# A decode kernel whose planner no longer puts filler matmuls into the two banks of the weighted sum

## The chip, the cores and the metric

The kernel runs on one core of a Trainium2 chip. The metric is the device time of one execution in microseconds. Three runs of the kernel before gave 1105.93, 1108.88 and 1117.53 us; their median, 1108.88 us, is the time before.

## What is computed

Eight batch rows, one token each, go twice through an attention layer A over a key and value cache and a small MLP block B, each with a residual sum. A's cache and weights are the same in both rounds.

```python
x = x + A(layernorm(x), k_cache, v_cache, wq, wo)
x = x + B(layernorm(x), w1, w2, w3, w4)
x = x + A(layernorm(x), k_cache, v_cache, wq, wo)
x = x + B(layernorm(x), w1, w2, w3, w4)
# A: q = x @ wq (16 heads of 256); k, v: [8 rows, 8 heads, 4096, 256], a head serves two query heads
#    p = softmax(q @ k.T / 16);  o = p @ v;  out = o @ wo
# B: h = gelu(layernorm(x) @ w1), shifted along the sequence in four groups, then @ w2 -> x1
#    x1 + gelu(layernorm(x1) @ w3) @ w4
```

All tensors are bf16; x is 8 x 448. The sequence has length one, so the shift in B brings in zeros alone, and the kernel reads neither w1 nor w2.

## The kernel before

**Data.** One head of one row has 2 MB of keys and 2 MB of values. Each such tile is cut into four quarters of 512 KB, with 128 partitions of 4 KB. The SBUF buffer `kv` has 30 places for quarters (`QUARTERS`). SyncE issues every load of keys and values (L622); one transfer brings one to four neighbouring quarters. A load waits until the last reader of each of its places is done. Between the two rounds of one row the kernel keeps the keys of five heads and six quarters of values on the chip, so these aren't read twice.

**A front and a back for each head.** `front` does the keys: TensorE transposes each half quarter with four fp32 transposes into one of the four PSUM banks psT0 to psT3 (L1219), VectorE or ScalarE copies the bank back over the same half quarter (L1202, L1203), and then the scores are made with the transposed keys as weights (L1037, 16 matmuls per quarter, the query column repeated to 48 columns). The maximum, the exponential and the sum follow on VectorE, GpSimd and ScalarE. `back` does the values: the weighted sum, eight matmuls per quarter (L1104), goes into columns 0 to 255 of one of two banks, psP0 and psP1, which the backs use in turn. VectorE then rounds the result and takes the remainder (L1118, L1120). A small matmul adds the four partial sums into columns 256 to 259 of the same bank (L1128), VectorE scales them to `oT` (L1134), and four matmuls multiply by the head's rows of wo (L1153). Columns 264 to 511 of psP0 and psP1 hold nothing that the result needs: here they are the upper halves.

**The stretch between a row's rounds.** After the last head of round one, a row goes through a chain that can't be split: psR to SBUF (L1163, L1165), the turn (L979, L982), the last head's product with wo, the sums of the norm, the MLP's two products (L833, then L979 and L982 again), the new queries (L817), and then the scores of round two. Meanwhile the values of the next row's three heads that keep nothing come in through the few places of `kv` that are free. The last two key quarters of head 7 don't stay in `kv`. They are held in transposed form in the four psT banks (`held_banks`, `HOLD = 2`), from their transposes in round one until head 7's scores in round two.

**The planner.** All work is listed as operations with durations, and `Plan.schedule` plays it through on a model: it orders each engine's instructions, gives places in `kv` to loads, and joins neighbouring quarters into one transfer. The order it finds is written out as the fixed instruction order of each engine, with semaphores. When the model finds TensorE idle, it may put in fillers: matmuls of the identity by itself, whose result nobody reads. They keep TensorE active. Over a sliding 3.413 us it aims at 3,500 columns (`TARGET`), and a filler is placed only where it is over before the next TensorE operation starts in the model. A filler needs a PSUM bank that is empty by the model's record, `bank_ev`: an operation with the attribute `tbank` set to a bank marks it occupied if it is a TensorE operation, and otherwise enters itself as the one that emptied it. Of the banks that are not occupied, the one that was emptied first is taken, and the filler waits for the operation that emptied it.

```python
b = [(x.end if x else -1.0, k) for k, x in bank_ev.items() if x is not True]
b = min(b, default=(1e9, 0))
if b[0] + 0.1 > u or u < 20.0:
    u += 0.1
    continue
f = self.filler(b[1])
...
if o.tbank is not None:
    bank_ev[o.tbank] = True if e == "pe" else o
```

For psT the marks are set in `transpose_piece`: occupied by the transposes, emptied by the copy, where a held piece's copy comes only in round two. For psP they are set in `back`: occupied by the first quarter's weighted sum, emptied by the operation that writes `oT`. The function `filler` makes 512 columns in a psT bank and 248 in the upper half of a psP bank. A bank that never gets a mark is never a candidate.

## Time and profile before

| | before |
|---|---|
| median of three runs | 1108.88 us |
| the profiled execution, its own time | 1107.5 us |
| its span, first to last instruction | 1105.7 us |
| mean granted TensorE clock | 0.927 |
| TensorE busy, of the span | 970.7 us, 88% |
| VectorE, ScalarE, GpSimd busy | 52%, 26%, 9% |
| HBM read | 438.38 MB, 396 GB/s over the span |
| DMA engines busy for the SyncE queue | 97.2% |
| fillers in the upper halves of psP | 184 of 248 columns, 35.6 us busy |
| fillers in psT | 42 of 512 columns, 14.5 us busy |

### The profile page before, as it was taken

To read this page: it belongs to the slowest core of one execution; us is meant where nothing else is said; L and a number is where in the kernel's file an instruction comes from. 1 tells how busy PE (TensorE), PEld (TensorE's weight loads), DVE (VectorE), ACT (ScalarE), POOL (GpSimd) and SP (SyncE) were. 2 spreads that over 40 slices of the span, in tenths; PEclk is the share of its full clock that TensorE was granted. 3 is DMA by queue.
4 is the path that set the end of the run, shared out by engine and by line. 5 is a ranking of instruction groups with operands and counts; after the bars stand their busy time and mean duration, and the time that the engine had idled before them with its cause. 6 is when DMAs were issued, how large, how long until landed. Compare 5 with 4: busy or idle time off the path is not lost.

```text
span 1105.7 us, 42629 instructions
## 1 busy us (share of the span) xinstructions
PE 970.7 (88%) x19504; PEld 775.8 (70%) x19504; DVE 572.6 (52%) x1782; ACT 287.7 (26%) x844; POOL 97.6 (9%) x275
## 2 busy tenths in 40 slices
PE   4889889898899988998988898998889898899987
PEld 4668657785678856786666865778567785688674
DVE  4345445554455544655544554565545655356644
ACT  1133113331224302242122321233112331234120
POOL 0000010010100101010000100100010100101010
PEclk9899989998899979999888989999979999799998
DMA  9999999999999999999999999999999999999994
GB/s 333 406 426 420 391 392 424 424 421 388 400 422 425 419 355 426 423 424 420 368 424 426 419 359 358 423 425 416 393 396 424 424 404 388 413 416 398 360 408 178
DMA packets 54543, 441.13 MB, mean 399 GB/s; under 512 B 5838, under 2 KB 9052, under 8 KB 27100
## 3 DMA queue, kind: packets, MB, share of 16 engines
q1 hardware_dynamic: 54356, 438.41, 97.2%
q8 instruction: 153, 2.51, 0.9%
q14 instruction: 26, 0.21, 0.0%
q10 hardware_dynamic: 8, 0.00, 0.0%
HBM read 438.38 MB, written 0.01 MB: 396 GB/s over the span
## 4 chain that ended last, share of the span: by engine, by line
PE 56%; DMA 32%; SPq 4%; issue 4%; DVE 3%; ACT 1%; POOL 0%
PE psT L1219 20%; DMA kv<-in_A_k_cache_dram 19%; PE psM L1037 16%; DMA kv<-in_A_v_cache_dram 13%; PE psP L1104 9%; SPq L622 4%; PE psR L1153 4%; PE psM L817 2%; PE psP L1424 1%; PE psP L1128 1%; PE psM L979 1%; DVE oS L1120 1%; DVE oS L1118 1%; PE psM L982 1%; ACT pT L1071 1%
## 5 line engine op out<-in xcount | busy, mean ns | idle before, releaser
L1219 PE MATMUL psT<-ident_f,kv 128*128 128x128 f32 x2816 | 388.6, 284 | 24.0 <-DMA kv<-in_A_k_cache_dram 23.3
L1202 DVE COPY kv<-psT 128x512 f32<-128x512 f32 x415 | 284.1, 690 | 176.5 <-PE psT L1219 170.0
L1219 PEld LDWEIGHTS psT<-ident_f,kv 128*128 128x128 f32 x2816 | 312.0, 144 | 48.4 <-DMA kv<-in_A_k_cache_dram 28.8
L1203 ACT COPY kv<-psT 128x512 f32<-128x512 f32 x321 | 186.5, 585 | 386.1 <-PE psT L1219 385.4
L1104 PE MATMUL psP<-kv,pT 128*2 128x256 bf16 x4096 | 187.5, 293 | 30.7 <-issue 16.9
L1037 PEld LDWEIGHTS psM<-q2T,kv 128*128 128x128 bf16 x4096 | 129.9, 100 | 46.7 <-issue 34.8
L1037 PE MATMUL psM<-q2T,kv 128*128 128x48 bf16 x4096 | 145.3, 189 | 13.2 <-issue 10.8
L1037 PEld LDWEIGHTS psM<-q1T,kv 128*128 128x128 bf16 x4096 | 134.3, 97 | 17.5 <-issue 11.2
L1037 PE MATMUL psM<-q1T,kv 128*128 128x48 bf16 x4096 | 143.2, 184 | 1.1 <-issue 0.4
L1104 PEld LDWEIGHTS psP<-kv,pT 128*2 128x2 bf16 x4096 | 79.1, 84 | 72.0 <-issue 27.3
L1071 ACT ACTIVATE pT<-sS,nb,fac 128x32 bf16<-128x32 f32 x128 | 52.7, 417 | 242.5 <-DVE nb L1065 242.5
L1061 POOL PARTITION_ALL_REDUCE gm<-pm x128 | 45.5, 355 | 758.3 <-DVE pm L1059 710.2
L1056 DVE COPY sS<-psM 128x64 f32<-128x64 f32 x128 | 28.5, 223 | 107.9 <-PE psM L1037 105.2
L1118 DVE CAST oS<-psP 128x256 bf16<-128x256 f32 x128 | 53.9, 421 | 51.4 <-PE psP L1104 49.2
L1153 PE MATMUL psR<-wo_sb,oT 128*1 128x448 bf16 x448 | 68.7, 390 | 5.0 <-DVE oT L1134 2.0
L1075 POOL PARTITION_ALL_REDUCE Db<-rs x128 | 51.0, 398 | 215.6 <-ACT pT L1071 215.6
L1128 PE MATMUL psP<-sel,oS 128*128 128x2 bf16 x512 | 32.4, 167 | 33.0 <-DVE oS L1120 29.2
L1128 PEld LDWEIGHTS psP<-sel,oS 128*128 128x128 bf16 x512 | 25.4, 100 | 49.8 <-DVE oS L1120 41.4
L1071 ACT ACTIVATE pT<-sS,nb 128x32 bf16<-128x32 f32 x128 | 40.9, 326 | 68.7 <-DVE nb L1065 68.7
L1120 DVE TENSOR_TENSOR oS<-psP,oS 128x256 bf16<-128x256 f32 x128 | 54.1, 423 | 3.5
L817 PEld LDWEIGHTS psM<-x2c,wq_sb 128*128 128x128 bf16 x768 | 30.7, 98 | 18.5 <-DVE sS L1056 6.1
L817 PE MATMUL psM<-x2c,wq_sb 128*128 128x24 bf16 x768 | 36.6, 184 | 5.0 <-issue 4.3
(159 smaller groups left out, 574.5 us busy)
## 6 DMA issues: line engine op xcount, KB each, us to landing
kv<-in_A_k_cache_dram SPq DMA_DIRECT2D x72, 2048.0 KB, 20.1
kv<-in_A_v_cache_dram SPq DMA_DIRECT2D x54, 2048.0 KB, 17.6
kv<-in_A_v_cache_dram SPq DMA_DIRECT2D x125, 512.0 KB, 7.5
kv<-in_A_v_cache_dram SPq DMA_DIRECT2D x54, 1024.0 KB, 10.7
kv<-in_A_k_cache_dram SPq DMA_DIRECT2D x23, 1024.0 KB, 12.2
kv<-in_A_v_cache_dram SPq DMA_DIRECT2D x5, 1536.0 KB, 10.2
kv<-in_A_k_cache_dram SPq DMA_DIRECT2D x12, 512.0 KB, 7.6
wo_sb<-in_A_wo_dram SPq DMA_DIRECT2D x1, 3584.0 KB, 45.5
```

Source lines behind the costliest of these rows:

```text
L817: last = t.matmul(bank[:, at + i * step:at + i * step + copies], w, r, start=(kc == 0), stop=(kc == 3))
L1037: last = t.matmul(ps[:, SB + 2 * i:SB + 2 * i + 2 * REP], a[:, c:256:2], bcast(rhs(c), REP, 1), start=(c == 0), stop=(c == 1))
L1071: return a.activation(pT[nr][:, :, :].rearrange("p i j -> p j i")[:, jj, :], sview[:, jj, :], ACT.Exp, bias=nb[nm][:, jj:jj + 1], scale=sc ...
L1075: plan.op("pool", lambda gp: gp.partition_all_reduce(Db[nr][:, :], rs[nr][:, :], P, RO.add), 0.5, "sum", rd=[("rs", nr, 0), ("rs", nr, 1)] ...
L1104: last = t.matmul(ps[g4:g4 + 2, PV0:PV0 + DH], pT[nr][:, i, :], slot_ap(q, s * 256, 256), start=(i < 4), stop=(i >= 28), skip_group_check= ...
L1118: plan.op("dve", lambda v: v.tensor_copy(oS[:, 0, :], po), 0.36, "o", rd=[("pv", par, x) for x in range(4)], wr=["oS0"], banks=[bk], prio=hi)
L1120: plan.op("dve", lambda v: v.tensor_tensor(oS[:, 1, :], po, oS[:, 0, :], ALU.subtract), 0.36, "o", rd=["oS0"] + [("pv", par, x) for x in r ...
L1128: last = t.matmul(ps[:, PV1 + 2 * c:PV1 + 2 * c + 2], oS[:, w, c:DH:2], sel[:, :], start=(w == 0), stop=(w == 1))
L1153: last = t.matmul(psR[r:r + 1, 0:D], oT[no][:, i % 2, i // 2:i // 2 + 1], wo_sb[:, a:a + D], start=(k == 1 and i < 2), stop=(k == HKV - 1 ...
L1202: return e.tensor_copy(dst, psT[bank][:, :])
L1203: return e.copy(dst, psT[bank][:, :])
L1219: last = t.transpose(psT[bank][:, s * P:(s + 1) * P], src, ident_f[:, :])
```

## The change

Both marks in `back` are taken away, so psP0 and psP1 never enter the planner's record of banks, and fillers can go only into psT0 to psT3. Nothing else is edited: the function `filler` still has its branch for psP, which is no longer reached. The schedule is made anew with the same model, targets and durations.

```diff
@@ back
                     wr=[("pv", par, x) for x in range(u, 4)], banks=[bk])
-            if u == 0:
-                o.tbank = bk
             if u not in keep_v:
                 o.frees = vs[u]
@@ back
         plan.op("dve", lambda v: v.tensor_tensor(
             oT[no][:, :, :], ps[:, PV1:PV1 + 4].rearrange("p (c j) -> p c j", c=2),
             bcast(rc[nr][:, :], 2, 1), ALU.mult), 0.16, "o", rd=[("o2", par), ("rc", nr)],
-            wr=[("oT", no)], banks=[bk], prio=hi).tbank = bk
+            wr=[("oT", no)], banks=[bk], prio=hi)
```

## The prediction

> **What bounds the kernel now.** I read the page's slices first, then the span cut into stretches, then the fillers, and last TensorE's own order around them. The page's slices and the chain that ended last:

> ```profile
> PEclk9899989998899979999888989999979999799998
> DMA  9999999999999999999999999999999999999994
> GB/s 333 406 426 420 391 392 424 424 421 388 400 422 425 419 355 426 423 424 420 368 424 426 419 359 358 423 425 416 393 396 424 424 404 388 413 416 398 360 408 178
> PE 56%; DMA 32%; SPq 4%; issue 4%; DVE 3%; ACT 1%; POOL 0%
> ```

> The DMA engines are busy nearly everywhere, yet the rate falls from some 424 to some 360 GB/s eight times, and the clock is low nearby. These are the stretches between the rounds of a row. Cut there, busy time of each engine, clock, DMA share and GB/s:

> ```profile
> 119.00:150.00 31.00, 26.87 (x587) 18.26 (x587) 13.42 (x60) 2.76 (x11) 1.15 (x3) 0.89 0.99 376
> 652.00:685.00 33.00, 27.50 (x598) 17.28 (x595) 15.77 (x70) 3.03 (x12) 1.86 (x5) 0.84 0.89 328
> 416.00:521.00 105.00, 92.46 (x1838) 77.25 (x1838) 58.07 (x155) 31.76 (x92) 10.90 (x29) 0.98 1.01 424
> ```

> The eight stretches (from 119, 257, 390, 521, 652, 786, 921 and 1023 us; 228 us in all) run at 360 GB/s on average, the seven between them (709 us) at 420. So 228 x (1 - 360/420) = 33 us of transfer are lost in the stretches, 1.9 to 7.2 us in each. Outside them the kernel is bound by transfers; inside, by how fast TensorE frees the few places for values. The change can only matter inside, because that is where the fillers are:

> ```profile
> L1424 PE MATMUL psP<-ident_f x184: 272/274/412, 119.4 to 1042.4; 128*128 128x248 bf16 x184
> ```

> ```profile
> L1424 PE MATMUL psP<-ident_f x43: 272/274/408, 119.4 to 140.8; 128*128 128x248 bf16 x43
> ```

> The second line is the first stretch alone. Cut as above, the filler line has 168 instructions in the eight stretches, all in psP: the 42 in psT stand before 119 us (24), after 1086 us (15) and three between.

> **Removed: are the fillers gone or moved?** In the first stretch the last transposes start at 114.75 us, and the next copies out of psT come at 147.5 to 149.1 us, on both engines, with no transpose between: all four psT banks are held. A held bank is marked occupied, so the planner has no bank at all and places nothing there. I count 168 of the 184 as gone. The 16 outside the stretches, in groups of one to three, can go to psT, at 512 columns where two of 248 stood; I cost that at nothing, since the transfers run at 420 GB/s there and cover TensorE, and at a filler's 0.1 to 0.2 us each, 3 us at most, if they didn't.

> **Removed: TensorE time.** A psP filler takes 9 per 1.20 us at full clock (row at 258.77), 10 per 2.25 us at half. That is some 20 to 35 us of TensorE, but nearly every group ends in a wait: the instruction after it starts within 0.05 us of the semaphore that it waits for, in all but a few of the groups. The clear exception:

> ```profile
> 522.64 2.25 PE L1424 MATMUL psP<-ident_f 128*128 128x248 bf16 x10
> 524.81 0.42 PE L1104 MATMUL psP<-kv,pT 128*2 128x256 bf16 x8
> ```

> Here the weighted sum waits for nothing but the fillers, 2.2 us. I take -2.0 us (bounds 0 and -3, with the few single fillers at 0.1 to 0.2 us).

> **Added: half-clock windows.** Cut on the clock's grid of 3.413 us, TensorE's idle time in a window stands against the clock of the next. Over the whole span, 20 windows have at least 1.5 us idle and 16 of them are followed by half clock; of the 260 with under 0.9 us, 21 are. Now two windows with fillers, as they are, and below them the fillers alone:

> ```profile
> 388.39:391.81 3.42, 2.61 (x30) 1.50 (x30) 2.09 (x7) 0.72 (x4) 0.40 (x1) 1.00 0.98 386
> 391.81:395.22 3.41, 2.55 (x69) 1.71 (x70) 1.17 (x4) 0.00 (x0) 0.00 (x0) 1.00 1.00 400
> ```

> ```profile
> 388.39:391.81 3.42, 1.69 (x12) 1.02 (x12) 1.00 0.98 386
> 521.51:524.93 3.42, 2.60 (x12) 1.29 (x10) 0.50 1.00 414
> ```

> Without fillers the window at 388.39 is idle for 3.42 - 2.61 + 1.69 = 2.5 us, and 391.81 should fall to half clock. The same sum gives 1.9 to 2.8 us at 118.74, 125.57, 255.27, 258.69, 521.51, 784.34 and 787.75, each followed by full clock today: eight candidates, at 16 in 20 some 6.4 new windows, 22 us at half clock on top of the 161 that the whole run has (twice the mean clock's shortfall, 2 x 0.073 x 1105.7). In the windows that follow stand 212 weighted-sum matmuls (0, 16, 32, 16, 40, 48, 20 and 40) and six matmuls of wo rows (L1153). The price of a weighted sum at the two clocks:

> ```profile
> 261.06 1.04 PE L1104 MATMUL psP<-kv,pT 128*2 128x256 bf16 x32 [0.35 <-DMA kv<-in_A_v_cache_dram]
> ```

> ```profile
> 659.54 1.88 PE L1104 MATMUL psP<-kv,pT 128*2 128x256 bf16 x32
> ```

> (1.88 - 1.04)/32 = 26 ns each, 5.5 us; four wo rows go from 0.54 us (258.29) to 0.91 us (521.79), so six cost 0.5. The MLP's product L833, 56 matmuls, takes 1.56 us at half clock (132.21) and 1.55 at full (529.72): nothing. Together 6.0 us if all is on the path, and 0 if waits for values hide it, as DMA waits hide much there. I take half: +3.0.

> [...]

> **Moved: the order.** The planner replays everything with a colder model clock, so loads can be cut and placed differently. The trace has no such second plan. The nearest rows are the stretches themselves, which do the same work in other orders: they lose 3.8, 4.1, 3.6, 7.2 and 3.7 us (from 257, 390, 521, 652, 786). The dear one:

> ```profile
> 654.63:658.05 3.42, 2.97 (x19) 0.50 0.92 352
> 658.05:661.46 3.41, 3.41 (x49) 0.50 1.02 418
> 661.46:664.87 3.41, 2.78 (x66) 1.00 0.13 55
> ```

> Clock, DMA share and GB/s end these lines. After two windows at half clock the weighted sums run late, no place comes free, and the transfers stop (0.13). One stretch turning from 3.6 to 7.2 costs +3.6; the bounds are -3.6 (that one mends) and +3.6 in each of seven. I take one: +3.6, since more half clock leans that way.

> **Sum.** 1107.5 - 2.0 + 3.0 + 3.6 = 1112.1 us for a profiled execution; with the 1.4 us by which the median stands above it, 1113.5 us, 0.4% slower. The three runs before spread over 1.0%, so a change within 1% (1098 to 1120) is about what cannot be told from none.

> **The rivals.**

> *Slower by more.* The stop of 661.46 becomes common: half clock in the stretch, weighted sums late, the free places not emptied, transfers standing. For it: in SyncE's waits, loads of L622 wait for weighted sums (L1104) 148 times, 373.6 us in all. Against: the stretches at 257, 390 and 521 have 10 to 14 us of half clock each (twice the shortfall of 0.80, 0.74 and 0.79) and no such stop. Full cold price, no gain from the fillers and three more such stretches: 1107.5 + 6.0 + 3 x 3.6 + 1.4 = 1126 us. It decides from two stops on with the full cold price: 6.0 + 7.2 is over 1%.

> [...]

> *It does nothing.* The planner finds psT banks after all in the stretches, and puts as many columns there: 1109 us. Against: the held banks, and no psT filler in any of the eight stretches.

> **How the numbers follow.** The forecast, up to 1% either way, has 0.42; slower by more 0.40; faster 0.12; nothing 0.06. Part of the forecast's own bounds reach over 1%, and the faster rival stands on the edge of it, so: faster by over 1% 0.11, within 0.47, slower 0.42. For the range: cold price 0 to 6, fillers 0 to -3, order -3.6 to +10.8 give 1102 to 1126 by the sum; the lower end goes 1 us further towards the faster rival and the upper to one stop more, 1130. One in ten is left out on each side.

> **What would show it.** The filler line should read some 40 to 60 instructions, all psT, none between 119 and 147 us. The clock in the eight stretches should fall by some 0.05 on average (now 0.74 to 0.95), the mean from 0.927 to some 0.917, and L833 stay at 1.55 us. The stretches' GB/s should stay within 328 to 390; a share under 0.2 in a window of a second or third stretch speaks for the slower rival, a gain in the stretches at 521 and 652 alone for the term of the fillers. I am wrong if fillers stand in the stretches, if the clock there doesn't fall, or if the loss comes outside the stretches, where only the new order could bring it.

## The result and the profile after

The change makes the kernel slower by 0.7%. Over 19 runs each, before has a median of 1110.38 us (1105.09 to 1117.53) and after 1118.04 us (1114.17 to 1123.20); the ratio is 1.0073 with a 95% interval of 1.0055 to 1.0091, so it lies inside the 1% that the prediction could not tell from no change, but clear of zero. In the middle that is 8.1 us. The profiled execution of after took 1120.72 us (span 1118.9 us), 2.7 us above its median, while that of before lay 2.9 us under its own: the two profiles differ by 13.2 us where the kernels differ by 8.1.

The page of after, its slices and its chain by engine:

```profile
PEclk9889799997899968999799988999799987998797
DMA  9999999999999999999999999999999989999894
GB/s 327 408 427 419 392 373 425 425 420 369 396 425 422 419 349 425 421 425 412 386 425 425 418 380 391 425 423 416 384 411 422 426 303 370 418 421 366 327 386 167
PE 57%; DMA 33%; issue 5%; DVE 3%; SPq 1%; ACT 1%; POOL 0%; DVEq 0%
```

The mean clock is 0.905 in this execution and 0.900 over all 19. The dips of GB/s stand where they stood, and there is a new one of 303 GB/s at slice 33. The filler line of after:

```profile
L1422 PE MATMUL psT<-ident_f x52: 385/408/628, 24.5 to 1114.7; 128*128 128x512 bf16 x52
```

All 184 fillers in psP are gone, and psT has ten more than the 42 of before. The same cuts as before, at fixed times (busy time of each engine, then clock, DMA share and GB/s):

```profile
119.00:150.00 31.00, 20.89 (x495) 14.55 (x496) 11.48 (x57) 1.75 (x9) 0.76 (x2) 0.67 0.96 361
652.00:685.00 33.00, 25.25 (x575) 16.89 (x572) 15.48 (x67) 2.79 (x11) 1.52 (x5) 0.74 0.97 360
416.00:521.00 105.00, 94.69 (x1897) 80.42 (x1893) 58.91 (x158) 33.55 (x98) 11.34 (x30) 0.97 1.01 419
```

The clock of the first stretch fell from 0.89 to 0.67, and in the row between stretches it hardly moved (0.98 before, 0.97 after). Fixed times drift against the work, so the stretches are better cut by the work itself: from the last transpose that fills the held banks to the first copy out of them. The sum line over the eight, of before and then of after:

```profile
sum 225.00, PE 194.06 PEld 125.40 DVE 108.67 ACT 16.12 POOL 8.95; mean PE 24.26 PEld 15.67 DVE 13.58 ACT 2.02 POOL 1.12
```

```profile
sum 235.30, PE 184.04 PEld 120.08 DVE 109.61 ACT 15.73 POOL 8.93; mean PE 23.01 PEld 15.01 DVE 13.70 ACT 1.97 POOL 1.12
```

The stretches take 10.3 us longer, and TensorE is busy 10.0 us less in them. Half-clock time inside them goes from 72 to 133 us: 21 windows of the clock's grid become 39 (the profile of before records 72 pieces of clock and that of after 66, and all but the last of each are whole multiples of 3.413 us long). The length alone overstates what a stretch costs, since a longer stretch also moves more bytes. By the prediction's own measure, length x (1 - rate/420), the eight stretches lose 29.8 us of transfers before and 32.9 after: 3.1 of the 13.2 us between these two executions. More is lost between two stretches, first before, then after:

```profile
815.00:921.00 106.00, 97.47 (x1968) 82.01 (x1963) 57.97 (x173) 33.40 (x96) 10.81 (x29) 0.95 1.00 416
815.00:921.00 106.00, 95.73 (x1900) 80.46 (x1895) 57.92 (x170) 32.63 (x94) 10.57 (x28) 0.94 0.96 392
```

By the same measure this is 1.0 us before and 7.1 us after. It holds the dip at slice 33, to which I come below. What half clock does in a stretch is seen in the first one of after, cut on this execution's grid:

```profile
121.20:124.61 3.41, 2.19 (x66) 2.00 (x66) 0.60 (x2) 0.00 (x0) 0.00 (x0) 0.50 0.94 385
124.61:128.03 3.42, 0.00 (x0) 0.00 (x1) 0.16 (x1) 0.00 (x0) 0.00 (x0) 0.50 0.98 409
128.03:131.44 3.41, 2.79 (x48) 1.30 (x48) 0.85 (x2) 0.00 (x0) 0.00 (x0) 0.50 1.00 397
131.44:134.85 3.41, 2.81 (x85) 2.10 (x82) 1.47 (x9) 0.00 (x0) 0.00 (x0) 1.00 1.07 409
134.85:138.27 3.42, 1.88 (x41) 0.98 (x38) 2.57 (x16) 0.21 (x1) 0.00 (x0) 0.50 1.03 427
138.27:141.68 3.41, 3.41 (x94) 2.94 (x92) 0.17 (x1) 0.00 (x0) 0.00 (x0) 0.50 0.82 329
141.68:145.09 3.41, 3.41 (x78) 2.50 (x78) 2.71 (x16) 0.00 (x0) 0.00 (x0) 0.50 0.83 286
```

Three windows at half clock follow each other, one of them without a single matmul. Before, fillers stood here and all of this up to 132.39 us ran at full clock. Three more follow from 134.85 us, and in the last two of them TensorE is busy throughout by its records: half clock goes on there although TensorE isn't idle. In the first three, the first weighted sums of the next head's values meet the half clock, in TensorE's timeline of after:

```profile
128.03 1.88 PE L1104 MATMUL psP<-kv,pT 128*2 128x256 bf16 x32 [3.43 <-DMA kv<-in_A_v_cache_dram]
```

1.88 us, where the same 32 took 1.04 us at full clock.

The dip at slice 33 lies outside the stretches, at the one place where the MLP of the finished rows is computed in a psT bank:

```profile
894.00:895.80 1.80, 0.02 (x1) 0.00 (x0) 0.33 (x2) 0.72 (x4) 0.48 (x2) 1.00 1.02 428
896.00:902.00 6.00, 6.00 (x64) 5.38 (x65) 1.65 (x4) 0.59 (x1) 0.00 (x0) 0.50 0.48 160
```

TensorE stands for 1.8 us with no wait that the profile shows, then transposes at half clock, and the transfers run half empty. Before had no filler at this place either, so this part of the profile doesn't come directly from a missing filler. Whether it belongs to the new order or to this execution can't be told from one profile.

### The profile page after: what moved, and what is told of

It is laid out like the page before. It is cut to its first block, busy times and chain, and to the rows that moved or that the text cites. A ratio compares the mean times of both kernels' runs of the same rounds, so it can differ in the third digit from the quotient of the medians.

```text
span 1118.9 us, 42270 instructions
## 1 busy us (share of the span) xinstructions
PE 956.4 (85%) x19330; PEld 767.2 (69%) x19330; DVE 578.0 (52%) x1786; ACT 286.1 (26%) x840; POOL 98.0 (9%) x275
## 4 chain that ended last, share of the span: by engine, by line
PE 57%; DMA 33%; issue 5%; DVE 3%; SPq 1%; ACT 1%; POOL 0%; DVEq 0%
PE psT L1217 23%; PE psM L1037 16%; DMA kv<-in_A_k_cache_dram 15%; DMA kv<-in_A_v_cache_dram 13%; PE psP L1104 9%; DMA wo_sb<-in_A_wo_dram 4%; PE psR L1151 3%; PE psM L817 2%; PE psM L979 1%; PE psM L982 1%; PE psP L1126 1%; DVE oS L1116 1%; ACT pT L1071 1%; DVE oS L1118 1%; PE psT L1422 1%
## 5 line engine op out<-in xcount | busy, mean ns | idle before, releaser
L1200 DVE COPY kv<-psT 128x512 f32<-128x512 f32 x419 | 287.4, 690 | 175.0 <-PE psT L1217 168.7
L1104 PE MATMUL psP<-kv,pT 128*2 128x256 bf16 x4096 | 195.0, 303 | 35.0 <-DMA kv<-in_A_v_cache_dram 21.1
L1037 PEld LDWEIGHTS psM<-q2T,kv 128*128 128x128 bf16 x4096 | 126.7, 99 | 54.1 <-issue 41.9
L1037 PE MATMUL psM<-q2T,kv 128*128 128x48 bf16 x4096 | 142.3, 187 | 23.0 <-issue 19.1
L1104 PEld LDWEIGHTS psP<-kv,pT 128*2 128x2 bf16 x4096 | 81.6, 86 | 84.2 <-DMA kv<-in_A_v_cache_dram 31.8
L1132 DVE TENSOR_TENSOR oT<-psP,rc 128x4 bf16<-128x4 f32 x128 | 20.2, 158 | 46.5 <-PE psP L1126 39.3
## 6 DMA issues: line engine op xcount, KB each, us to landing
kv<-in_A_v_cache_dram SPq DMA_DIRECT2D x5, 1536.0 KB, 10.8
```

What stands on the lines that cost most here:

```text
L1037: last = t.matmul(ps[:, SB + 2 * i:SB + 2 * i + 2 * REP], a[:, c:256:2], bcast(rhs(c), REP, 1), start=(c == 0), stop=(c == 1))
L1104: last = t.matmul(ps[g4:g4 + 2, PV0:PV0 + DH], pT[nr][:, i, :], slot_ap(q, s * 256, 256), start=(i < 4), stop=(i >= 28), skip_group_check= ...
L1200: return e.tensor_copy(dst, psT[bank][:, :])
```

## The experiments

Two theories stood against each other. **Clock**: without fillers the stretches run colder, and that costs the time in any order. **Order**: the new schedule costs it, and the clock is innocent. A third, **fetch**, says that the position of the instructions in the fetched stream matters (the page of before lists 153 packets of instructions with 2.51 MB on queue q8). All ratios are to before on the same chip, with five rounds each.

**The old order without fillers.**

```diff
     plan.schedule()
+    gone = [o for o in plan.order["pe"] if o.name == "warm" and o.dur[2] == 248]
+    plan.order["pe"] = [o for o in plan.order["pe"] if o not in gone]
+    plan.ops = [o for o in plan.ops if o not in gone]
     plan.synchronise()
```

> The schedule of before, with the 184 fillers in the upper halves left out when the order is written down; nothing else moves. If the colder clock is what costs (theory clock), this is slower than before by most of the 0.7% of the change, some 1116 to 1118 us, with a mean clock near the 0.905 of after. If the new order is what costs (theory order), it stays within 0.2% of before, some 1108 to 1112 us, at the same low clock. If the fillers cost TensorE time (rival faster), it is below 1107 us.

Measured: 1.0067 (1.0033 to 1.0101), median 1117.94 us, mean clock 0.894. Leaving out the fillers alone, with nothing reordered, brings nearly the whole of the change. Its profile shows its slowest run (1129.97 us) and isn't read further.

**The old order with narrow fillers.**

```diff
         def warm(t):
-            return t.matmul(dst, ident_b, bcast(ident_b[:, 0:n // 4], 4, 1), start=True,
-                            stop=True)
+            w = n if n == 512 else 4
+            return t.matmul(dst[:, 0:w], ident_b, bcast(ident_b[:, 0:w // 4], 4, 1), start=True,
+                            stop=True)
```

> As before, with the 184 fillers in their places in the order but 4 columns wide in place of 248: the instruction count and the place of every instruction in the stream stay, the array's activity goes. Theory clock: as slow as the run without the fillers, within 0.2%. If what matters is not the activity but where the instruction stream is cut into fetched blocks (theory fetch): as before, 1110 us, while the run without fillers differs. Theory order: both stay at 1110 us.

```profile
L1425 PE MATMUL psP<-ident_f x184: 166/167/189, 119.6 to 1050.7; 128*128 128x4 bf16 x184
```

Measured: 1.0045 (1.0025 to 1.0066), clock 0.896. The filler line shows all 184 in place with their weight loads, but with 4 columns each they don't hold the clock: 0.896, beside 0.894 without any and 0.929 with 248 columns. The time is lost although no instruction moved: fetch is out as the main cause. The profile of this run shows best where the loss lies, since every instruction has its place of before. Its first stretch, to be set beside the first row at 119 us that the prediction shows (clock 0.89, 376 GB/s):

```profile
119.00:150.00 31.00, 23.47 (x547) 16.47 (x548) 12.16 (x57) 2.17 (x10) 0.99 (x3) 0.61 0.95 352
```

Cut by the work, its eight stretches take 234.0 us for 225.0, with 154 us of half clock for 72, and lose 39.6 us of transfers for 29.8. These 9.8 us are as much as the whole difference of the two executions (1116.97 and 1107.5 us), which is larger than that of the kernels (0.45%, 5.0 us). Whether the 0.2% by which it is better than the run without any filler is real can't be said; the intervals overlap.

**The new order with fillers.** A second record holds the marks of psP (`pbank`), and where no psT bank is open, fillers are put in by the same target without the model's knowledge.

```diff
+            if e == "pe" and self.filler and t - free["pe"] > 0.1 and \
+                    all(x is True for x in bank_ev.values()):
+                u = max(free["pe"], t - 3.0)
+                while u + 0.22 <= t + 0.06:
...
+                    f = self.filler(b[1])
+                    f.deps[bank_p[b[1]]] = False
+                    f.pos = len(order["pe"])
+                    order["pe"].append(f)
```

> The schedule of after, to which fillers of 248 columns in the upper halves are added wherever the planner had no transposing bank, without the model seeing them: the order of the real work and the loads are those of after. Theory clock: back to 1110 us, clock back to 0.92 or more. Theory order: stays at 1117 to 1119 us although the clock comes back.

Measured: 1.0042 (1.0023 to 1.0061), clock 0.926, with 183 fillers. It falls between the two theories: the mean clock comes back, and less than half of the time (0.31% of 0.73%) with it. Read alone, this would say that the order costs 0.4%. But the mean over the whole run hides that the stretches are still colder: in the profile they have 97 us of half clock, where before has 72 and after 133.

**More fillers, new schedule.** One constant, `HOT = 3500` to `HOT = 5000`.

> Before with HOT = 5000 in place of 3500, the planner's column target from the eve of a held stretch to the second round's first scores: more fillers there, a new schedule. Theory clock: fewer half-clock windows in the stretches and 0 to 5 us less than before, 1105 to 1110 us. Theory order: any change of the schedule moves the time by some us either way, whatever the clock does.

Measured: 1.0046 (1.0022 to 1.0070), clock 0.941, 267 fillers in psP. A warmer clock than before (0.929), and slower: above the level of before, a warmer clock alone doesn't make this kernel faster. The schedule is a new one, so this run doesn't say whether its order or its fillers cost the time.

**Four draws of the order.** How much an order matters by itself was asked by changing a number of the planner's model by less than a per cent, twice with fillers and twice without.

```diff
-    BLOCK, FETCH = 128, 6.0
+    BLOCK, FETCH = 128, 6.02
```

```diff
-    ISSUE, LEAD = 4.0, 5.0
+    ISSUE, LEAD = 4.02, 5.0
```

> The kernel before (fillers in the upper halves) with one number of the planner's model changed by 0.3%, the time between two fetched blocks from 6.0 to 6.02 us. It should change nothing by itself but the order that comes out. Theory clock alone: within 0.2% of before, 1108 to 1113 us. Theory order (before's own order is a lucky draw, any other order costs some 0.4%): 1113 to 1118 us at an unchanged clock of 0.92 or more.

> The kernel before with another number of the model changed by 0.5%, the delay of a load's issue from 4.0 to 4.02 us: a second draw of an order with fillers. Theory clock alone: 1108 to 1113 us. Theory order: 1113 to 1118 us.

> The kernel after (no fillers in the upper halves) with the fetch number changed from 6.0 to 6.02 us: a second draw of an order without fillers. If missing fillers cost by themselves some 0.3% on top of an average order, this lies at 1115 to 1120 us, above both draws with fillers; if only the order counts, it lies among them.

> The kernel after with the issue delay changed from 4.0 to 4.02 us: a third draw of an order without fillers. If missing fillers cost by themselves, 1115 to 1120 us at a clock near 0.90; if only the order counts, among the draws with fillers.

Measured, with fillers: 0.9987 (0.9965 to 1.0010) and 1.0014 (0.9992 to 1.0036). Without: 1.0079 (1.0048 to 1.0111) and 1.0082 (1.0054 to 1.0110). By these draws before's order is no lucky one, and after's no unlucky one among those without fillers.

**Fillers in the orders made without them, and out of one made with them.** The edits above, joined with the changed numbers.

> The order of the draw without fillers whose fetch number is 6.02, with unseen fillers added as in the run of the new order with fillers. If fillers are worth the same 0.7% whatever the order, it comes to within 0.2% of before, 1107 to 1112 us, and the order of after is an unlucky one. If an order made with a colder model costs 0.4% by itself, 1113 to 1116 us again.

> The same with the issue number 4.02: a third order made without fillers, with unseen fillers added. 1107 to 1112 us if the order of after was unlucky; 1113 to 1116 us if the colder model's orders are worse.

> The order of the draw with fillers whose fetch number is 6.02, which ran at 1108 us, with the fillers of the upper halves left out when it is written down. If the missing fillers cost the same in any fixed order, 1115 to 1118 us; if before's own order was peculiar, less than 0.3% over its own 1108 us.

Measured: 1.0021 (0.9998 to 1.0043), 1.0011 (0.9991 to 1.0031) and 1.0074 (1.0048 to 1.0099). With these, five orders have been run both ways:

| order | with fillers | without | missing fillers cost |
|---|---|---|---|
| before's | 1.0000 | 1.0067 | 0.67% |
| with fillers, fetch 6.02 | 0.9987 | 1.0074 | 0.87% |
| after's | 1.0042 | 1.0073 | 0.31% |
| without, fetch 6.02 | 1.0021 | 1.0079 | 0.58% |
| without, issue 4.02 | 1.0011 | 1.0082 | 0.71% |

The mean cost is 0.63%. Without fillers every order lies between 0.67% and 0.82% over before, whatever model made it. With fillers, orders made by the colder model come to 0.11% to 0.42%, of which only after's own is clear of zero. The stretches show the same in the second pair, first with fillers, then without:

```profile
654.60:683.30 28.70, 24.92 (x537) 15.87 (x536) 13.80 (x63) 1.95 (x9) 1.11 (x3) 0.82 0.95 359
...
sum 227.20, PE 196.25 PEld 128.38 DVE 109.42 ACT 16.03 POOL 8.86; mean PE 24.53 PEld 16.05 DVE 13.68 ACT 2.00 POOL 1.11
```

```profile
653.50:682.00 28.50, 23.32 (x516) 15.15 (x515) 13.72 (x63) 1.93 (x9) 1.11 (x3) 0.70 0.94 357
...
sum 233.30, PE 186.04 PEld 123.47 DVE 109.31 ACT 16.25 POOL 8.86; mean PE 23.26 PEld 15.43 DVE 13.66 ACT 2.03 POOL 1.11
```

The eight stretches grow by 6.1 us and lose 4.0 us more of transfers, and the two spans differ by 5.0 us (1110.4 and 1115.4): between these two executions most of the loss lies in the stretches. Their medians differ by more, 0.87% or 9.7 us. Not every stretch grows (the one shown doesn't, at a clock of 0.70 in place of 0.82).

**The old order with still more fillers.**

```diff
                     if sum(x[1] for x in recent) > (self.HOT if hot else self.TARGET):
+                        ...
+                        if b[0] + 0.1 <= u and sum(x[1] for x in recent + extra) < 5000:
+                            f = self.filler(b[1])
+                            f.deps[bank_ev[b[1]]] = False
+                            f.pos = len(order["pe"])
+                            order["pe"].append(f)
                         u += 0.1
                         continue
```

> The schedule of before to the instruction, with further fillers of 248 columns in the upper halves that the model does not see, up to 5,000 columns per 3.4 us instead of 3,500. If each us at half clock in the stretches costs the same 0.1 us all the way, this gains some 3 us, 1106 us, at a clock of 0.94. If the gain is used up at the level of before (the stretches wait for values then), 1109 to 1111 us. If fillers begin to stand in the way of weighted sums, above 1112 us.

```profile
L1437 PE MATMUL psP<-ident_f x414: 272/274/408, 55.0 to 1106.8; 128*128 128x248 bf16 x138
```

Measured: 1.0028 (1.0002 to 1.0055), clock 0.945. With 414 fillers for 184 the clock gains 0.015 over before on the same chip (0.930), and the time gains nothing; it is slightly worse. Only about half of the added fillers stand in the stretches, and half-clock time there falls little, from 72 to 61 us; the rest of the clock's gain lies outside, where transfers bind (DMA share 1.01 at 424 GB/s in the row of before from 416 us). So this run shows that more fillers of this kind bring nothing; what a much warmer stretch would be worth in the same order stays untested. No version was found that is clearly faster than before.

## Why the prediction was right, and where its steps were not

The direction, the size class and the range held: 1113.5 us forecast against 1118.04 us measured, in a range of 1101 to 1130. The sum came out 4.5 us short (1.5 us of it because the three runs of before had a lower median than the 19), and two of its three terms were wrong. That it came so near is partly luck: the term for the order, which the runs don't bear out, made up for a term for the clock that was too small. Without the order term the forecast would have been 1 us over before, where 8.1 us were measured.

**Gone or moved: right.** None of the 168 fillers of the stretches was moved; the 52 that remain are all in psT, and the first stretch has none. The rival that the change does nothing falls with that.

**Half-clock windows: the right mechanism, a third of the size.** "Eight candidates, at 16 in 20 some 6.4 new windows, 22 us" was the step that failed. Half-clock time took 32% of the stretches before and 57% after, so their clock fell by 0.12 where the prediction expected 0.05. The profiles show 18 more windows in the stretches, 61 us; by the mean clocks (0.929 over the 28 runs of before beside the first experiments, 0.900 over the 19 of after) the whole run has 66 us more, twice the shortfall times the span. I counted windows in which the clock would newly begin to fall, each lasting one window. But the falls are hardly more: 14 pieces at half clock touch the stretches before, 15 after. They last longer, 21 windows in 14 pieces before and 39 in 15 after, and 45 in 11 with the narrow fillers in before's order. Counted per window, both changed: of the full-clock windows that touch the stretches 14 of 52 were followed by half clock before and 15 of 36 after, of the half-clock windows 7 of 21 and 24 of 39. The windows that stay at half clock aren't simply empty: in 17 of these 24 TensorE was idle for less than 0.9 us. What keeps the clock low in them, the narrow or the slow matmuls in them for instance, wasn't tested. The longest pause of TensorE in after's stretches, the 3.43 us shown above, came when the clock had already fallen, at 121.20 us, after a window in which TensorE was idle for 2.2 us.

**The price of half clock: right in size, in part by luck.** The prediction took 3.0 us for 22 us, 0.136 us each; measured are 8.1 us for 66 us, 0.123 each. But the 3.0 was the middle between 0 and 6, taken without a row that shows how much is hidden, and the price isn't fixed: with narrow fillers in before's order it is 5.0 us for 73 us, 0.07 each. The row of 1.88 us for 32 weighted sums returned to the digit, and the 56 matmuls of L833 stayed as they were (1.47 to 1.49 us from the first start to the last at half clock in after, 1.43 to 1.47 at full in before).

**The order, +3.6 us: wrong.** With fillers, a new draw moved the time by -0.13% and +0.14%; without them, old and new order cost 0.67% and 0.73%. For this change the term should have been near zero, as far as intervals of some 0.2 to 0.3% to either side can tell. The stretch at 652 us, which I took for the price of a bad order, lost less in the new order: 33 x (1 - 360/420) = 4.7 us instead of 7.2.

**The fillers' own time, -2.0 us: not seen.** Taking them out of a fixed order gained nothing that can be seen beside the loss. That fillers can stand in the way is suggested by the two runs with more of them, which are slower at a warmer clock (1.0046 at 0.941, 1.0028 at 0.945); the size for the 184 stays open.

**The rivals.** *Faster*, which had 0.12, falls: the page of before gives the fillers (PE psP L1424) 1% of the chain that ended last, some 11 us, but before's own order without them took 0.67% more, so that was no time to be had. *Slower by more* was half right: the transfers do stop, at 1049 to 1053 us in after (share 0.29), and at 896 to 902 us, which no stretch holds; but in the profiles of the three other orders without fillers the transfers mostly pause for a microsecond or less at a time, with one longer pause near 1048 us. One sign of being wrong that the prediction named, a loss outside the stretches, came in the profile of after (6.1 of 13.2 us between 815 and 921 us); in before's order with narrow fillers the loss lies in the stretches.

**What stays open.** Why after's own order keeps 0.42% when it gets its fillers back, where two like it keep 0.1% and 0.2%, isn't settled. The stop at 896 us explains a part at most. In the profile of that run the 6 us from 896 us go at 388 GB/s instead of 160, and the time between the two stretches around it (817 to 925 us) loses 4.1 us of transfers, where the same part loses 1.3 before and 7.3 after. Its eight stretches lose 32.6 us, 2.8 more than before's, while the two spans differ by 7.8 us. In all three of these runs the fillers are placed without the model's knowledge, unlike before's; what that costs isn't known.

## What to carry to other kernels

Where filler work holds the clock up, as here (0.929 with the fillers, 0.894 without them in the same order), count how long the low clock lasts when the fillers go, not only how often it begins: here the falls stayed about as many (14 and 15 pieces), and the half-clock windows nearly doubled (21 and 39). Look at the clock in the stretches that depend on it, and not only at its mean over the run. Price the low clock by the instructions that it slows down and by who waits for them, since 32 weighted sums (256 columns) went from 1.04 to 1.88 us here, and the narrow matmuls of L833 (24 columns) lost hardly anything, under 0.1 us in 56 of them. And when a planner makes a new order, run two or three orders that differ by a rounding before blaming or praising the order.

## What the runs showed of the hardware

184 fillers of 4 columns with their full weight loads of 128 columns (102 ns each) didn't hold the clock: the mean clock of the runs is 0.896 with them, 0.894 without any, 0.929 with 248 columns. So the weight loads alone brought 0.002 here; the rest came with the streamed columns or with the time they take (274 ns for 248 columns, 167 for 4), which no run tells apart. A window with a pause of 1.8 us stood before the two half-clock windows that begin near 896 us, and the second of them came although TensorE was busy throughout the first (6.00 of 6.00 us from 896 us, each matmul counted to its modelled end).
